# Block-sparse attention followed by a GELU layer pair: the second layer of batch 0 by seven products, casts moved between engines, and a new order of all instructions

## The chip, the cores and the metric

The kernel runs on one core of a Trainium2 chip. The core has five engines that each work through their own instructions in order: TensorE (PE in the profile) multiplies matrices into PSUM, VectorE (DVE) and ScalarE (ACT) do elementwise work, GpSimd (POOL) does elementwise work and issues some transfers, and SyncE (SP) issues most transfers. Sixteen DMA engines move data between the chip's memory and the on-chip buffers. Engines wait for each other by semaphores. The metric is the device time of one execution in microseconds; lower is better.

## The reference

The inputs are q, k and v with 4 batches, 8 heads, 768 positions and 64 dimensions, and two weight matrices, w_in (512 x 2048) and w_out (2048 x 512), all in float32.

First comes attention in which each position sees only some blocks of 64 keys. For every query the mean key of each of the 12 blocks gives a score; the three best blocks that are not in the future, and the query's own block, are kept. Inside them the mask is causal, and a softmax over the kept scores weighs the values:

```
k_rep = k.reshape(B, H, n_blocks, block, D).mean(axis=3)
gate_scores = np.einsum('bhsd,bhnd->bhsn', q, k_rep)
top_idx = np.argsort(gate_scores, axis=-1)[..., -top_k:]
scores = scale * np.matmul(q, k.transpose(0, 1, 3, 2))
```

The heads of a position are put side by side (512 numbers), which gives x with 3072 rows. Two layers follow: h = x @ w_in, g = the tanh form of GELU of h, and out = g @ w_out.

## The kernel before

The work goes batch by batch; one batch is 768 positions. Within a batch the heads are taken in pairs, p = 0 to 3 for batch 0 and 4 to 15 for batches 1 to 3.

**Preparing a pair** (`pre`, called by `prepare`). For batches 1 to 3 a pair's keys and queries are loaded by four transfers each (`load`, L427), in a layout that VectorE's 32 x 32 block transpose (L585) turns into dimension by position. For the keys VectorE then sums each block (L628) and makes ksb from the sums (L645). Keys and queries are cast to 16 bits per head by `copy`, whose lines are L391 on ScalarE, L393 on GpSimd and L395 on VectorE. TensorE multiplies queries by ksb (the gate, L693); VectorE transposes the result (L709) and selects the three best blocks (L716, L725, L726, L730). The resulting mask is transposed, by TensorE (L762) for batches 0 and 1 and by a transfer (L769) after that, and copied into extra rows of the queries, so that a score product adds the mask by itself.

**Attention of a pair** (`heads2` for batch 0, `heads` for the others). Per head and pair of key blocks, TensorE computes scores (L866 for batch 0, L1049 later), ScalarE takes the exponential (L885, L1062), GpSimd clears what lies in the future on the diagonal (L911, L1076), and TensorE multiplies by the values (L934, L1088). VectorE divides by the sums, and the result is turned into xT, by TensorE (L991) or a transfer (L996).

**First layer** (`s1`). For each of 16 groups (j, h), eight matmuls of 384 columns (L1124) give a tile of h, and ScalarE writes its GELU into G (L1136). G is stored as four quarters A11, A12, A21, A22: by halves of the hidden dimension and of the positions.

**Second layer.** For batches 1 to 3, `s2` computes G times w_out as a 2 x 2 block product with seven products of blocks in place of eight. VectorE makes sums of the quarters of G (`sums`, L1194, four for each of four slices c, into XS and, in place, A21) and of the quarters of w_out (`w_sums`, L1176, into TS and, in place, B12). For each of three token tiles TensorE runs seven products of eight matmuls with 256 columns (L1254), and VectorE combines them with five copies and additions (L1298). For batch 0, `s2_plain` computes the product directly: six token tiles of 16 matmuls with 512 columns (L1206), each copied out once by VectorE or ScalarE. Since `w_sums` changes w_out in place, its sums wait for batch 0's direct products.

**Buffers that share memory.** The first loads of batch 0 land in memory that G and TS use later, and 16-bit keys, queries and masks of batch 0 lie in XS. `early` lists what must be done before G and TS are written.

**What sets the order.** The kernel does not emit its work as written. Each piece is an `Op` with the engines that it may use and an estimated duration on each, its dependencies, the buffers that it takes and gives, and a priority. `Plan.solve` walks through time with these estimates, picks among the pieces that can start soonest the one of best priority, and chooses the engine that would end it first. The list `RANK` replaces all priorities by position. The planner's estimates decide the order only; on the chip every engine runs its own order and waits where a result is not there yet.

**Warming matmuls** (`warm`, L1401). 72 matmuls on the identity matrix, whose results nobody uses, take the lowest priority. The planner puts them where, by its estimates, TensorE would have nothing else to do.

**Weights and queues.** GpSimd issues w_in and w_out in two halves each (`load_w`, L485), each first half behind a tiny copy (L482) that waits for a certain load. SyncE has tiny loads (`hold`, L493) that wait until the first half of w_in, and later of w_out, has landed; the loads of pair 4's queries and keys stand behind the first, the other loads of batch 1 behind the second. The last operation in the kernel's own text that bears on the change is this:

```
s1(0)
s2_plain(0)
w_sums()
```

Of the kernel before, what the change touches and what calls it, by code (L numbers as in the profile page):

```python
# [21 lines left out]
    143, 420, 146, 147, 145, 418, 121, 260, 475, 56, 260, 228, 112, 261,  # L22
    587, 70, 261, 497, 19, 324, 5, 4, 324, 6, 2, 323, 8, 631, 1, 326, 32,
    54, 326, 31, 24, 324, 16, 758, 3, 329, 20, 42, 329, 13, 337, 326, 40,
    367, 372, 329, 30, 355, 38, 955, 1277, 846, 49, 934, 948, 573, 141, 248,
    583, 1191, 645, 590, 118, 241, 117, 242, 240, 198, 61, 119, 83, 613,
    108, 900, 357, 89, 751, 650, 150, 88, 253, 252, 148, 388, 1017, 1315,
    1018, 986, 109, 50, 36, 362, 473, 27, 204, 130, 22, 28, 712, 129, 23,
    21, 832, 236, 135, 265, 286, 124, 209, 428, 151, 520, 230, 325, 351,
    954, 235, 327, 350, 901, 624, 328, 433, 1099, 552, 310, 939, 305, 97,  # L30
    375, 529, 318, 882, 317, 417, 374, 889, 330, 285, 363, 287, 69, 233,
    595, 174, 137, 595, 90, 176, 339, 384, 339, 95, 111, 256, 898, 581, 441,
    280, 110, 897, 629, 923, 227, 474, 352, 298, 258, 543, 921, 62, 259,
    660, 142, 626, 829, 316, 510, 131, 216, 710, 276, 160, 26, 187, 282,
    321, 366, 189, 526, 208, 277, 533, 257, 185, 949, 431, 429, 494, 430,
    577, 331, 268, 641, 278, 838, 381, 625, 273, 289, 320, 462, 237, 465,
    369, 461, 730, 171, 464, 359, 341, 436, 458, 264, 358, 348, 1512, 269,
    456, 364, 398, 937, 213, 432, 361, 365, 360, 864, 460, 251, 219, 639,
    281, 354, 272, 347, 909, 234, 535, 344, 899, 340, 338, 370, 307, 127,
    218, 760, 387, 373, 243, 217, 791, 98, 379, 378, 945, 353, 186, 839,  # L40
    416, 478, 371, 776, 523, 956, 380, 138, 591, 524, 175, 343, 229, 488,
    170, 349, 801, 445, 840, 482, 12, 199, 65, 491, 595, 309, 564, 37, 79,
    85, 80, 84, 713, 17, 1128, 1069, 1232, 283, 284, 1228, 43, 41, 134, 313,
    1093, 1138, 1143, 1171, 755, 9, 559, 314, 400, 579, 288, 477, 466, 476,
    522, 15, 415, 444, 446, 521, 11, 1071, 504, 413, 1094, 25, 585, 512,
    602, 592, 94, 1070, 621, 841, 1072, 7, 593, 530, 528, 642, 14, 489,
    1114, 1319, 484, 10, 578, 414, 409, 485, 39, 493, 471, 454, 499, 18,
    549, 859, 861, 560, 34, 684, 734, 952, 1073, 35, 636, 596, 1102, 677,
    48, 496, 857, 447, 486, 29, 1235, 1257, 1269, 1286, 165, 1248, 778, 990,
    1198, 1220, 1217, 1218, 1223, 308, 203, 291, 211, 190, 715, 721, 1230,  # L50
    51, 172, 1226, 1266, 503, 565, 534, 681, 767, 676, 576, 822, 678, 652,
    653, 759, 770, 786, 612, 536, 911, 787, 792, 793, 800, 916, 917, 1043,
    1249, 126, 125, 222, 293, 295, 303, 292, 300, 226, 158, 689, 690, 736,
    743, 817, 836, 965, 404, 195, 192, 391, 395, 545, 546, 702, 423, 201,
    757, 421, 424, 425, 377, 691, 693, 718, 762, 735, 563, 495, 479, 505,
    541, 519, 619, 1124, 487, 194, 1237, 729, 246, 247, 245, 244, 249, 498,
    584, 427, 383, 604, 795, 794, 1061, 1213, 412, 746, 630, 932, 1321, 440,
    434, 270, 91, 907, 401, 768, 123, 634, 63, 796, 720, 104, 212, 798, 802,
    651, 675, 1040, 72, 724, 896, 46, 1044, 919, 254, 605, 223, 1039, 106,
    615, 294, 667, 744, 178, 668, 774, 924, 597, 68, 1329, 597, 87, 662,  # L60
    597, 173, 205, 52, 53, 81, 82, 77, 396, 76, 773, 989, 531, 86, 78, 918,
    74, 107, 385, 144, 221, 386, 159, 816, 664, 225, 356, 844, 833, 177,
    977, 392, 163, 692, 183, 782, 834, 301, 181, 154, 940, 835, 179, 740,
    393, 164, 705, 402, 538, 890, 335, 599, 103, 156, 599, 115, 169, 599,
    132, 162, 33, 73, 601, 616, 666, 459, 71, 688, 513, 483, 665, 719, 845,
    149, 255, 197, 188, 399, 502, 196, 714, 302, 567, 166, 726, 722, 304,
    206, 622, 75, 394, 506, 128, 717, 716, 306, 224, 765, 723, 290, 220,
    707, 403, 514, 673, 764, 537, 698, 262, 600, 96, 550, 600, 140, 334,
    600, 116, 167, 64, 555, 994, 974, 161, 263, 553, 544, 202, 184, 500,
    501, 728, 297, 59, 210, 279, 518, 152, 312, 1127, 618, 122, 1274, 1216,  # L70
    623, 136, 319, 1214, 406, 1126, 480, 368, 322, 733, 139, 1260, 457,
    1215, 938, 271, 470, 114, 661, 410, 1019, 155, 935, 481, 953, 927, 933,
    1264, 603, 790, 812, 903, 566, 250, 930, 902, 654, 426, 606, 725, 761,
    699, 1666, 872, 1341, 883, 1541, 1060, 1023, 992, 1062, 1645, 928, 904,
    922, 942, 1373, 950, 1063, 1088, 1007, 1178, 711, 685, 814, 819, 1663,
    1542, 92, 448, 905, 1067, 655, 1090, 1101, 1547, 818, 913, 910, 929,
    1394, 1064, 1032, 1029, 1068, 1139, 1056, 1053, 975, 1097, 1182, 468,
    451, 453, 925, 1049, 1013, 1059, 1066, 885, 1006, 1001, 875, 876, 101,
    1225, 914, 1356, 1425, 1275, 1100, 1112, 1255, 1227, 1137, 467, 442,
    881, 912, 1098, 1492, 1494, 1491, 1469, 1579, 1649, 804, 450, 463, 1144,  # L80
    1675, 1766, 1751, 1459, 1605, 1609, 1607, 920, 1689, 1688, 1278, 1389,
    1452, 1468, 1641, 1710, 961, 1680, 1660, 1683, 1697, 967, 737, 749, 100,
    1696, 1754, 1009, 1011, 784, 1031, 1033, 1016, 1025, 1024, 1020, 1132,
    1095, 1045, 1131, 1140, 1146, 1147, 1046, 1221, 1262, 1276, 1263, 777,
    750, 1239, 1241, 1080, 659, 656, 772, 1243, 1083, 695, 979, 57, 779,
    783, 1118, 1160, 754, 1158, 1219, 1298, 1324, 886, 1014, 1440, 1516,
    669, 511, 382, 469, 443, 1209, 570, 753, 868, 1152, 1245, 1314, 703,
    1409, 1538, 1424, 1421, 1461, 1458, 1672, 113, 267, 105, 180, 982, 1771,
    200, 982, 1772, 232, 982, 1775, 342, 299, 58, 60, 207, 67, 539, 93, 828,
    452, 397, 66, 969, 527, 848, 1351, 870, 133, 588, 1642, 1156, 988, 1212,  # L90
    1700, 1606, 991, 1429, 1699, 1698, 1092, 1057, 1010, 1048, 1608, 727,
    1581, 1455, 1578, 1177, 1244, 1532, 1496, 1175, 960, 1602, 936, 617,
    968, 1183, 1366, 1047, 157, 983, 1769, 231, 983, 1768, 756, 983, 1770,
    311, 405, 120, 274, 275, 438, 532, 408, 657, 1234, 492, 906, 435, 542,
    849, 866, 865, 644, 878, 1580, 1206, 1258, 1681, 1390, 1065, 1291, 1701,
    1682, 1194, 1159, 1740, 1026, 1717, 1190, 1419, 1021, 1661, 908, 803,
    1117, 1456, 1106, 1236, 1121, 999, 620, 998, 1089, 996, 1406, 830, 984,
    1773, 558, 984, 1774, 594, 984, 1776, 1489, 411, 437, 1724, 1723, 449,
    407, 873, 877, 884, 1332, 1204, 871, 389, 850, 966, 1005, 419, 895,
    1008, 1353, 1304, 1261, 1224, 1290, 915, 658, 1012, 1203, 1355, 780,  # L100
    1085, 1129, 855, 888, 1240, 1022, 1229, 1523, 1242, 1145, 856, 887, 788,
    1084, 825, 1030, 1289, 860, 1113, 747, 985, 1778, 556, 985, 1777, 540,
    985, 1767, 748, 1331, 1323, 1515, 1514, 1345, 820, 1346, 1526, 957, 962,
    1352, 1326, 731, 853, 1081, 1082, 672, 1252, 607, 1551, 1335, 1015,
    1201, 1561, 507, 1438, 1120, 1256, 1313, 1483, 1125, 1310, 1322, 1312,
    571, 1296, 1325, 1433, 785, 1437, 1119, 1420, 752, 1055, 1155, 1671,
    1259, 1493, 568, 569, 1270, 1272, 1422, 1684, 697, 831, 808, 869, 1611,
    943, 947, 1037, 1036, 1079, 813, 811, 810, 944, 1728, 1674, 1704, 1695,
    1714, 1104, 993, 1096, 1179, 1736, 1115, 1189, 1135, 1136, 1726, 1300,
    1308, 1306, 1318, 1676, 1170, 1168, 1165, 1172, 1721, 1207, 1635, 980,  # L110
    976, 1038, 1111, 1105, 1103, 562, 1233, 1148, 1163, 1281, 1544, 1134,
    1133, 1161, 1166, 1722, 1173, 1002, 1091, 1162, 1693, 1707, 963, 964,
# [167 lines left out]
def kernel(  # L280
# [9 lines left out]
    nc = tc.nc  # L290
    B, H, S, D = q.shape
    NBLK = S // 64
    NC = S // 128
# [8 lines left out]
    NG = 2 * (NC - 1)  # L302
    HALF = S // 2
    HD = DM // 2
    FAST = range(1, B)
    NCOLD = 18
    LAND = 3.0
    TURN = {"k": (), "q": (2, 3), "v": ()}
# [1187 lines left out]
```

## Time and profile before

| what | value |
|---|---|
| median of 3 runs | 259.65 us (258.12 to 259.68) |
| the profiled execution's own time | 259.51 us |
| its span | 257.8 us |
| TensorE busy | 250.8 us, 97%, 2530 matmuls |
| VectorE busy | 179.6 us, 70% |
| ScalarE busy | 165.2 us, 64% |
| GpSimd busy | 86.3 us, 33% |
| direct products of batch 0 (L1206) | 96 matmuls, 25.8 us busy |
| key and query casts on GpSimd (L393) | 21, of 0.862 us |
| query casts on VectorE (L395) | 15, of 0.590 us |
| query casts on ScalarE (L391) | 9, of 0.829 us |
| sums of G's quarters (L1194) | 48, of 0.55 to 0.57 us |

The span is the time from the first to the last instruction of the profiled execution; some 1.7 us lie around it. Busy time of TensorE counts overlapping matmuls once, so the mean duration of one matmul (0.379 us for 512 columns) is longer than the distance between two of them; what a stretch of matmuls costs is read from stretches in the timeline or in the chain of waits. In the stages of the run, batch 0's heads take until about 39 us, its first layer until 63 us, the heads of batch 1 with batch 0's second layer until about 99 us, batch 1's first layer until 124 us, and so on by batch; batch 3's second layer ends the run.

### The profile page before, as it was taken

How to read it: one execution, taken by the hardware profiler on the slowest of the kernel's cores; microseconds unless marked ns; L12 is line 12 of the kernel's file. 1: busy time of each engine (PE TensorE's matmuls, PEld its weight loads, DVE VectorE, ACT ScalarE, POOL GpSimd, SP SyncE). 2: the span in 40 equal slices, each digit the busy share in tenths (PEclk: the TensorE clock that was granted, in tenths of full speed). 3: DMA queues.
4: the chain of work that ended last, by engine and by line, in shares of the span. 5: the costliest groups of instructions: out<-in, count | busy, mean ns of one | idle time of the engine just before them, and what ended most of it. 6: DMA issues, size and time to landing. Idle time of an engine off the chain costs nothing.

```text
span 257.8 us, 6491 instructions
## 1 busy us (share of the span) xinstructions
PE 250.8 (97%) x2530; PEld 174.8 (68%) x2530; DVE 179.6 (70%) x523; ACT 165.2 (64%) x207; POOL 86.3 (33%) x169
## 2 busy tenths in 40 slices
PE   6799999998999999999999999999999999999997
PEld 5676776564556556556678876556778796667886
DVE  2887863318478999999999999997844462227552
ACT  2359688564789996565989587565898953664000
POOL 8754834003355676223043835100143310000000
DMA  8997898999969997899599694222011152000222
GB/s 159 218 152 161 152 215 132 186 225 185 206 132 212 161 196 159 154 188 174 86 206 194 113 215 99 66 69 51 1 75 42 41 104 83 3 0 0 84 81 84
DMA packets 134095, 32.63 MB, mean 127 GB/s; under 512 B 127696, under 2 KB 130096, under 8 KB 134064
## 3 DMA queue, kind: packets, MB, share of 16 engines
q1 hardware_dynamic: 129328, 27.62, 54.5%
q0 software_dynamic: 3136, 4.19, 10.0%
q10 hardware_dynamic: 1600, 0.39, 0.8%
q8 instruction: 20, 0.33, 0.5%
q14 instruction: 11, 0.09, 0.1%
HBM read 27.26 MB, written 6.29 MB: 130 GB/s over the span
## 4 chain that ended last, share of the span: by engine, by line
PE 71%; DMA 11%; DVE 7%; SPq 7%; ACT 2%; issue 2%; POOL 0%; DVEq 0%; ACTq 0%
PE bank L1254 21%; PE wide L1124 18%; PE wide L1049 10%; PE bank L1206 7%; SPq L427 6%; PE bank L1088 6%; DMA ksd<-in_k_dram 5%; DMA w_in<-in_moe_w_in_dram 4%; PE bank L1401 3%; PE bank L693 2%; DMA qsd<-in_q_dram 2%; PE wide L866 1%; ACT at L885 1%; PE bank L566 1%; DVE sel L725 1%
## 5 line engine op out<-in xcount | busy, mean ns | idle before, releaser
L1124 PE MATMUL wide<-xT,w_in 128*128 128x384 f16 x512 | 87.2, 326 | 0.1
L1136 ACT ACTIVATE G<-wide 128x768 f16<-128x768 f32 x64 | 51.8, 810 | 41.7 <-PE wide L1124 41.7
L1124 PEld LDWEIGHTS <-w_in 128*128 128x128 f16 x512 | 49.3, 98 | 33.2 <-issue 1.9
L1062 ACT ACTIVATE at<-wide 128x896 f16<-128x896 f32 x72 | 63.3, 917 | 10.5 <-PE wide L1049 8.1
L1076 POOL TENSOR_SCALAR_AFFINE_SELECT at<-at 128x256 f16<-128x256 f16 x72 | 31.1, 433 | 66.4 <-ACT at L1062 65.9
L1049 PE MATMUL wide<-qT,kT 76*128 76x512 f16 (+3 forms) x192 | 38.7, 305 | 0.0
L393 POOL CAST kT<-k 64x768 f16<-64x768 f32 x21 | 18.1, 862 | 37.4 <-DVE k L585 30.4
L1254 PE MATMUL bank<-w_out,G 128*128 128x256 f16 x216 | 30.0, 272 | 0.0
L1254 PEld LDWEIGHTS <-G 128*128 128x128 f16 x288 | 26.9, 98 | 4.1
L1298 DVE TENSOR_TENSOR osb<-bank,osb 128x512 f32<-128x512 f32 (+1 forms) x38 | 22.5, 596 | 8.8 <-PE bank L1254 8.2
L1206 PE MATMUL bank<-w_out,G 128*128 128x512 f16 x96 | 25.8, 379 | 0.0
L1088 PEld LDWEIGHTS <-at 128*128 128x128 f16 x504 | 21.6, 98 | 4.3 <-POOL at L1076 0.4
L885 ACT ACTIVATE at<-wide 128x1024 f16<-128x1024 f32 (+3 forms) x24 | 20.8, 917 | 5.5 <-PE wide L866 5.4
L1049 PEld LDWEIGHTS <-kT 76*128 76x128 f16 x192 | 17.5, 98 | 9.7
L1088 PE MATMUL bank<-v,at 128*128 128x65 f16 x504 | 23.8, 194 | 0.0
L1254 PEld LDWEIGHTS <-XS 128*128 128x128 f16 x216 | 20.3, 98 | 3.1 <-issue 0.3
L1254 PE MATMUL bank<-TS,XS 128*128 128x256 f16 x144 | 20.6, 272 | 0.0
L585 DVE STREAM_TRANSPOSE k<-ksd 128x768 f32<-128x768 f32 x12 | 11.6, 969 | 10.2 <-DMA ksd<-in_k_dram 10.2
L1194 DVE TENSOR_TENSOR XS<-G 128x768 f16<-128x768 f16 x12 | 6.5, 550 | 15.2 <-ACT G L1136 15.0
L1401 PE MATMUL bank<-ident 128*128 128x256 f16 x72 | 12.8, 302 | 2.1 <-DVE ident L323 2.1
L972 DVE TENSOR_TENSOR xn<-bank,zr 128x384 f16<-128x384 f32 x24 | 13.4, 558 | 0.8
L1206 PEld LDWEIGHTS <-G 128*128 128x128 f16 x96 | 8.7, 98 | 7.6 <-issue 1.0
(97 smaller groups left out, 322.8 us busy)
## 6 DMA issues: line engine op xcount, KB each, us to landing
out_dram<-osb SPq DMA_DIRECT2D x23, 256.0 KB, 2.0
vsd<-in_v_dram SPq DMA_DIRECT2D x26, 192.0 KB, 3.2
qsd<-in_q_dram SPq DMA_DIRECT2D x48, 96.0 KB, 2.5
ksd<-in_k_dram SPq DMA_DIRECT2D x48, 96.0 KB, 2.5
w_in<-in_moe_w_in_dram POOLq DMA_DIRECT2D x2, 1024.0 KB, 10.7
w_out<-in_moe_w_out_dram POOLq DMA_DIRECT2D x2, 1024.0 KB, 12.5
G<-in_k_dram SPq DMA_DIRECT2D x4, 192.0 KB, 4.6
G<-in_v_dram SPq DMA_DIRECT2D x4, 192.0 KB
```

The costliest lines, as they stand in the source:

```text
L393: nc.gpsimd.tensor_copy(out=out, in_=in_)
L885: nc.scalar.activation(out=T["at", u][:, :, 0:n], in_=plan.buf[("st",) + u].rearrange("p (h w) -> p h w", h=2)[:, :, 0:n], func=AF.Exp, bi ...
L1049: nc.tensor.matmul(st[:, x:e], kT16[i][h][0:76, s0:s0 + 128], qT16[i][h][0:76, s0 + (x - cb):s0 + (e - cb)], start=True, stop=True)
L1062: nc.scalar.activation(out=T["at", u][:, 0:n], in_=plan.buf[("st",) + u][:, 0:n], func=AF.Exp, bias=0.0, scale=SCALE)
L1076: nc.gpsimd.affine_select(out=dg, in_=dg, compare_op=ALU.is_ge, fill=0.0, base=0, pattern=[[0, 2], [1, 128]], channel_multiplier=-1)
L1088: nc.tensor.matmul(pvv[:, qc, 0:65], at[:, cb + (qc - jc) * 128: cb + (qc - jc + 1) * 128], v16[i][:, jc, h, :], start=(gi == 0 and jc == ...
L1124: nc.tensor.matmul(hps[:, 512 * e:512 * e + HALF], w_in16[:, ci, (2 * j + e) * 128: (2 * j + e + 1) * 128], T["xT", b][:, ci, HALF * h:HAL ...
L1136: nc.scalar.activation(out=G[:, :, h, j, :], in_=plan.buf["hps", b, j, h].rearrange("p (e w) -> p e w", e=2)[:, :, 0:HALF], func=AF.Gelu_a ...
L1206: nc.tensor.matmul(plan.buf["ops", b, ti], G[:, f % 2, 2 * ti // NC, f // 2, ti % (NC // 2) * 128:ti % (NC // 2) * 128 + 128], w_out16[:, ...
L1254: nc.tensor.matmul(dst[:, HD * h:HD * h + HD], FACT[m][0][:, j, t * 128:(t + 1) * 128], FACT[m][1][:, j, :], start=(clear and j == 0), sto ...
L1298: nc.vector.tensor_tensor(out=dst(), in0=src(), in1=other(), op=ALU.add)
L1401: nc.tensor.matmul(plan.buf["warm", n][:, 0:256], ident16, z, start=True, stop=True)
```

## The change

The second layer of batch 0 is computed by `s2`, as for the other batches. `s2_plain` goes, with the set `FAST` that kept the sums of G's quarters to batches 1 to 3, and the list `plain` that made the sums of w_out's quarters wait. These sums and batch 0's sums get priorities near the end of batch 0's first layer. In batches 1 to 3 key casts may run on GpSimd alone (before: VectorE or GpSimd), query casts on ScalarE or GpSimd (before: VectorE or ScalarE). `RANK` is another list, longer by 13, so all engines get a new order.

```diff
-    FAST = range(1, B)
...
-            kcs = [add({DVE: 0.56, POOL: 0.85}, kc_all(h),
+            kcs = [add({POOL: 0.85}, kc_all(h),
                        [t, old.get("k", None)], pr + 0.1) for h in range(2)]
...
-            q16s = [add({DVE: 0.56, ACT: 0.84}, q16(h), qcs + [old.get("s")],
+            q16s = [add({ACT: 0.84, POOL: 0.85}, q16(h), qcs + [old.get("s")],
                         pr + 0.1) for h in range(2)]
...
-            if j % 2 and h and b in FAST:
-                sums(b, j // 2)
+
+        for c in range(NJ // 2):
+            sums(b, c)
...
                 prev = w_sum[m, x] = add(
-                    {DVE: 0.66}, emit, [w_ready["out", x], prev] + early + plain.get(x, [])[-1:],
-                    1600 + x)
+                    {DVE: 0.66}, emit, [w_ready["out", x], prev] + early, 590.5 + 0.1 * x)
...
             prev = a_sum[b, m, c] = add(
                 {DVE: 0.55}, emit, g + [prev, x_free.get((b - 1, m, c))],
-                1000 * b + 600 + 4 * c)
-
-    def s2_plain(b):
...
+                1000 * b + 600 + 4 * c if b else 594 + 0.1 * c)
...
     s1(0)
-    s2_plain(0)
     w_sums()
+    s2(0)
```

In the new order the engines hold these instructions more or fewer than before: TensorE 168 products of 256 columns in place of 96 of 512; VectorE 16 sums of G's quarters and 12 additions of outputs more, 15 query casts, 3 key casts and 2 output copies fewer; GpSimd 13 query casts and 3 key casts more; ScalarE 2 query casts more. Lines below L305 have moved: in the changed file the sums of G's quarters are L1193, the products L1212, the additions of outputs L1256 and the warming matmuls L1359.

## The prediction

> **What bounds the kernel now.** I read the page's busy times first, then a table of busy time by stage, then the chain of waits, then TensorE's timeline around the change.
>
> In the table by stage the columns are: from and to, length, then busy time (and instructions) of PE, weight loads, DVE, ACT and POOL, then granted clock, DMA share, GB/s.
>
> ```profile
> PE 250.8 (97%) x2530; PEld 174.8 (68%) x2530; DVE 179.6 (70%) x523; ACT 165.2 (64%) x207; POOL 86.3 (33%) x169
> ...
> 39.00:63.00 24.00, 22.82 (x176) 13.88 (x173) 9.04 (x27) 14.99 (x19) 4.28 (x7) 1.00 1.16 178
> ...
> 68.00:97.00 29.00, 29.00 (x308) 16.94 (x307) 25.06 (x79) 26.02 (x34) 17.05 (x31) 1.00 0.90 180
> 97.00:124.00 27.00, 26.86 (x210) 15.76 (x209) 26.34 (x75) 16.98 (x24) 9.78 (x12) 1.00 0.87 161
> ```
>
> From 63 us on TensorE has practically no idle time; that is where the changed products lie. So work taken from TensorE there shortens the run, and a wait put there lengthens it one for one. VectorE is nearly as full from 97 us. Before 63 us there is one wait that counts:
>
> ```profile
> 43.30 13.99 DMA ksd<-in_k_dram
> 57.28 0.02 issue
> 57.31 0.99 DVE k L585
> 58.30 0.02 issue
> 58.32 0.95 DVE ks L628
> 59.28 0.46 DVE kT L395
> 59.74 0.73 DVE ksb L645
> 60.47 0.04 issue
> 60.51 0.48 PE bank L693 x8
> ...
> 63.38 3.24 PE bank L1206 x15
> ...
> 214.41 20.80 PE wide L1124 x128
> ...
> 237.18 13.32 PE bank L1254 x122
> ...
> 254.32 2.18 PE bank L1401 x20
> ```
>
> This is the chain of waits (start, length, what). The first keys of batch 1 land only at 57.3 us, 14 us after their last transfer is issued, because both halves of w_out (issued at 42.3 and 43.2 us, landed 10.5 and 14.5 us later) share the DMA engines. VectorE then needs 3.2 us until ksb, and only then can the gate product of pair 4 (L693) run. In TensorE's timeline that gate shows its wait:
>
> ```profile
> 60.51 0.48 PE L693 MATMUL bank<-q,ksb 128*32 128x160 f32 x8 [1.18 <-DVE ksb L645]
> ```
>
> TensorE works in order, so everything behind the gate waits too. Here 114 of the 128 matmuls of batch 0's first layer stand ahead of it; they hide all but 1.18 us.
>
> **The change, part by part.** The base is the profiled execution itself, 259.51 us (span 257.8); the median of the runs shown is 259.65, so I add to 259.5 and read the sum as the median. Positions come from the order of instructions on each engine in the two kernels.
>
> *Products.* Removed: 96 matmuls of 512 columns at 3.24/15 = 0.216 us, 20.74 us. Added: 168 of 256 columns at 13.32/122 = 0.1092 us, 18.34 us. Effect **-2.4 us**, on the path.
>
> *Warming matmuls* (L1401, 2.18/20 = 0.109 us each). 72 in both, but they move. Before, 20 stand behind the last real matmul, where they cost nothing. After, none does. Behind the gate of pair 4 and ahead of the last product stand 8 before and 26 after: 18 x 0.109 = **+2.0 us**. Three more stand in the first layer ahead of the gate; they lie in its wait and cost nothing.
>
> *Place of the gate.* In the new order 92 first-layer matmuls stand ahead of pair 4's gate, not 114. The 22 that moved behind it take 22 x 20.80/128 = 3.58 us. The gate's wait hid them; now TensorE reaches the gate at about 60.51 - 1.18 - 3.58 + 0.33 = 56.1 us and stands until ksb. Since the time of the gate is set by the keys, **+3.6 us** of work now lies behind it.
>
> *From keys to ksb.* Two of batch 0's factor sums (L1193 in the new file, 0.55 us) now stand between the transpose and ksb, a key cast (0.46) leaves, and ksb itself took 0.73 here, 0.15 elsewhere. Between -0.5 and +1; I take **+0.2**.
>
> *When the keys land.* The chain goes back to w_in's first half: issued by GpSimd at 27.06, landed at 36.3, then the small load that holds the queue, then queries, then keys. In the new order GpSimd reaches that issue one affine select, the cast of pair 3's queries and pair 2's value cast later. That query transpose ended at 28.7 here, so at this trace's times the issue would be 3.3 us late (28.7 + 2 casts of 0.82 = 30.4); VectorE's earlier part is somewhat shorter (two 0.48 us mask copies go to ScalarE). A better order of loads could also gain, by no more than the hole of some 1.5 us that the DMA engines have before 27 us. Ends -1.5 and +3.3; I take **+1.0**.
>
> *Clock after the wait.* TensorE would stand some 5 us. The row nearest to that is the start: after 2.07 us idle the first 14 warming matmuls took 3.17 us, 0.226 each, not 0.109. Against it, an idle time of 1.46 us at 10.3 us left the next warming matmuls at full speed. Ends 0 and 14 x 0.117 = 1.6; I take **+0.8**, the middle, as neither row is near 5 us. The Trainium skill ("TensorE: Matmul & The Clock Gate", Part 1) says the clock halves after an idle window of about 3.4 us and returns after as long a busy one, which would make it the full 1.6 or a little more. No row here shows a wait of that length.
>
> *Start of the seven products.* While VectorE waits for the keys, 14 of the 16 factor sums and all 8 weight sums (0.64 to 0.69) are queued behind that transpose. After ksb at 60.7 VectorE owes 4 sums (2.2), the selection of pair 4 (L709 to L730, 2.0), 8 weight sums (5.3) and 7 sums (3.8): 74.0 us. TensorE meanwhile has 36 first-layer matmuls (5.9), 38 products (4.2), 5 score groups (1.9), 21 value matmuls (0.6), masks, gate and 13 warming ones (2.1) until it needs the last of these, 75.2 us. In total enough, but product 5's third and fourth quarters and product 6's last come due just before their sums: waits of 0.4, 0.6 and 0.3 by adding up the rows. Ends 0 and 3; I take **+1.0**.
>
> *Later pairs.* From pair 5's gate to pair 6's VectorE has norms and joins 2.0, selection 2.0, transposes, sum, mask copy and ksb 3.4: 7.4 us. TensorE has 34 products (3.7), value and score matmuls 1.7, masks 0.3, warming 0.3 and the gate 0.4: 6.5. So 0.9 us idle; from pair 6 to 7 it is even. **+0.9**, ends 0 and 3. The casts taken from VectorE are already out of these numbers.
>
> *What costs nothing.* 18 casts (15 query, 3 key) leave VectorE, about 11 us, 16 sums and the joins of three tokens come, about 16 us less 1.4 for two output copies. TensorE has no idle time after 63 us that a faster VectorE could remove, so the relief gains nothing. GpSimd has 33% busy and takes 16 casts of 0.86, 14 us, beside them; that cover is questioned below.
>
> Sum: -2.4 + 2.0 + 3.6 + 0.2 + 1.0 + 0.8 + 1.0 + 0.9 = +7.1; 259.5 + 7.1 = **266.6 us**.
>
> **Rivals.**
>
> *The keys come early (no change, 259.8).* If SP issues the first queries and keys without the 2.88 us stall that its row shows at 38.67, the keys' packets are through before w_out's begin; a key load's median landing is 2.5 us. If they land by 52.5 us (56.1 less 3.2 of VectorE, with slack), the gate waits for nothing: -2.4 products, 21 x 0.109 = +2.3 warming, -1.2 for the old wait, +1.0 and +0.9 as above, less 0.3 for sums begun earlier, +0.3. Against it: the order queries, keys, w_out is the same as now, where they did not slip ahead. 15%.
>
> *GpSimd blocks VectorE (269.5).* Small VectorE operations stretch beside GpSimd's casts:
>
> ```profile
> 112.11 0.28 DVE L726 TENSOR_TENSOR sel<-sel,sel 128x120 f32<-128x120 f32 x1
> ...
> 118.33 0.98 DVE L726 TENSOR_TENSOR sel<-sel,sel 128x120 f32<-128x120 f32 x1
> ```
>
> The second ran beside key and value casts on GpSimd (117.44 to 120.0). Four query casts and a key cast more fall between 60 and 97 us, each able to hold up VectorE by about 0.7: up to 3 us more, where TensorE waits for VectorE: 266.6 + 2.9. For the milder case: VectorE's own casts go. The Trainium skill ("SBUF — State Buffer", Who interferes with whom) states an exclusive lock: a VectorE operation with two inputs in SBUF waits for the whole of a GpSimd instruction that reads SBUF. By it the factor sums and selections would each wait up to 0.8 us. 18%.
>
> *Faster (256).* The first: keys early, and the heads of batch 0 also end 2 us sooner, so that the first layer starts at 37.5 instead of 39.6, and the sums find VectorE idle (it has 9.0 of 24 us busy before 63 us): 259.8 - 2.1 - 1.9 = 255.8. 5%. That the change does not remove what it says is out: the orders show it.
>
> **How the numbers follow.** Forecast 62%, its own range 262.5 to 268.5 (clock, landing and start at their low or high ends together). With the early keys (258.5 to 261.5) cut at 260 and the blocked VectorE to 270, the range is 260 to 270; about 2 in 10 is left out. Bounds of 1%, about what a measurement of this kernel can tell, are 257.1 and 262.2: faster 5%; same 15% from early keys and 3% from the forecast's edge; slower the rest, 77%.
>
> **What would show it.** Right: TensorE's timeline has a wait of 4 to 6 us before pair 4's gate with 36 first-layer matmuls behind it; 168 products at 0.109 us; warming matmuls among batch 0's products; none after the last. The keys land near 58 us. Wrong: the keys landing before 53 us, which takes away 5 us of the sum at once; or an order of the first 39 us that brings w_in several microseconds sooner.

## The result and the profile after

The changed kernel takes 270.47 us (median of 4 runs, 270.09 to 271.74) against 259.44 for the kernel before (4 runs), a ratio of 1.0445 with a 95% interval of 1.0393 to 1.0496: slower, and 3.9 us above the 266.6 us that were predicted. Some executions of a kernel are slower at a lower granted clock; the ratios here leave them out, the medians do not. The profiled execution took 270.09 us (span 268.4), 10.58 more than the one before; the prediction's sum was 7.1.

The page of the changed kernel, its busy times and the granted clock in 40 slices of 6.7 us:

```profile
PE 251.5 (94%) x2602; PEld 182.2 (68%) x2602; DVE 184.1 (69%) x532; ACT 165.4 (62%) x207; POOL 97.6 (36%) x185
...
PEclk9999999995999999999999999999999999999999
```

TensorE is busy for the same time as before (251.5 and 250.8 us) in a span that is 10.6 us longer, and one slice, at about 63 us, ran at half the clock. What ends and follows the wait, in TensorE's timeline (start, length, instruction, in brackets the wait):

```profile
62.35 0.76 PE L693 MATMUL bank<-q,ksb 128*32 128x160 f32 x8 [7.69 <-DVE ksb L645]
63.05 3.74 PE L1124 MATMUL wide<-xT,w_in 128*128 128x384 f16 x12
66.62 0.60 PE L1212 MATMUL bank<-w_out,G 128*128 128x256 f16 x4
```

Pair 4's gate (0.48 us before) waits 7.69 us in place of 1.18, and the 12 first-layer matmuls behind it take 3.7 us where 12 x 0.1625 = 1.95 is their usual time. The chain of waits says what was late (start, length, what), and VectorE's timeline shows the last stretch of it:

```profile
28.80 8.21 DMA w_in<-in_moe_w_in_dram
...
44.59 13.55 DMA ksd<-in_k_dram
```

```profile
58.17 0.98 DVE L585 STREAM_TRANSPOSE k<-ksd 128x768 f32<-128x768 f32 x1 [8.95 <-DMA ksd<-in_k_dram]
59.07 0.52 DVE L1193 TENSOR_TENSOR XS<-G,XS 128x768 f16<-128x768 f16 x1
59.51 0.94 DVE L628 TENSOR_REDUCE ks<-k 128x12 f32<-128x768 f32 x1
60.36 1.20 DVE L1193 TENSOR_TENSOR G<-G 128x768 f16<-128x768 f16 x1
61.49 0.80 DVE L645 TENSOR_TENSOR ksb<-bmask,ks 128x32 f32<-128x32 f32 x1
```

The keys land 0.86 us later than before, and from there to ksb VectorE needs 4.15 us in place of 3.2: two factor sums stand between, and the second, 0.55 us elsewhere, takes 1.20 while GpSimd casts keys (59.21 to 61.16). So the gate is 1.84 us later than before, and the other 8.7 us arise behind it. Of those, 1.44 us are waits between 63 and 97 us (all from 86.4 us on, ahead of score matmuls), and 1.63 us are waits that lie much later, in batch 2's heads. There the table by stage reads, before and then after (from and to, length, busy time and instructions of PE, weight loads, DVE, ACT and POOL, clock, DMA share, GB/s):

```profile
135.00:168.00 33.00, 33.00 (x385) 24.79 (x384) 31.84 (x90) 23.82 (x31) 15.21 (x27) 1.00 0.71 135
```

```profile
135.00:168.00 33.00, 31.37 (x391) 24.61 (x389) 31.55 (x79) 25.43 (x32) 22.32 (x40) 1.00 0.83 157
```

### The profile page after: what moved, and what is told of

Read it like the earlier page. It is cut to its first block, busy times and chain, and to the rows that moved or that the text cites. A ratio compares the mean times of both kernels' runs of the same rounds, so it can differ in the third digit from the quotient of the medians.

```text
span 268.4 us, 6671 instructions
## 1 busy us (share of the span) xinstructions
PE 251.5 (94%) x2602; PEld 182.2 (68%) x2602; DVE 184.1 (69%) x532; ACT 165.4 (62%) x207; POOL 97.6 (36%) x185
## 4 chain that ended last, share of the span: by engine, by line
PE 69%; DMA 8%; DVE 7%; POOL 6%; ACT 3%; SPq 3%; issue 3%; POOLq 0%; DVEq 0%; ACTq 0%
PE wide L1124 26%; PE bank L1212 24%; PE wide L1049 7%; DMA ksd<-in_k_dram 5%; PE bank L1088 4%; DMA w_in<-in_moe_w_in_dram 3%; SPq L427 2%; PE bank L693 2%; ACT at L1062 2%; PE bank L1359 1%; PE wide L866 1%; DVE ks L628 1%; POOL at L1076 1%; DVE ksb L645 1%; POOL kT L393 1%
## 5 line engine op out<-in xcount | busy, mean ns | idle before, releaser
L1124 PE MATMUL wide<-xT,w_in 128*128 128x384 f16 x512 | 89.0, 330 | 0.0
L1212 PE MATMUL bank<-w_out,G 128*128 128x256 f16 x288 | 40.6, 272 | 0.0
L1212 PEld LDWEIGHTS <-G 128*128 128x128 f16 x384 | 36.1, 98 | 6.3 <-issue 0.3
L1256 DVE TENSOR_TENSOR osb<-bank,osb 128x512 f32<-128x512 f32 (+1 forms) x50 | 29.7, 599 | 13.4 <-PE bank L1212 12.7
L393 POOL CAST kT<-k 64x768 f16<-64x768 f32 x24 | 20.4, 850 | 26.0 <-DVE k L585 20.3
L1212 PEld LDWEIGHTS <-XS 128*128 128x128 f16 x288 | 26.6, 97 | 4.1 <-issue 0.5
L1212 PE MATMUL bank<-TS,XS 128*128 128x256 f16 x192 | 27.5, 272 | 0.0
L1193 DVE TENSOR_TENSOR XS<-G 128x768 f16<-128x768 f16 x16 | 9.5, 592 | 22.6 <-ACT G L1136 22.3
L585 DVE STREAM_TRANSPOSE k<-ksd 128x768 f32<-128x768 f32 x12 | 11.6, 969 | 9.0 <-DMA ksd<-in_k_dram 9.0
L1359 PE MATMUL bank<-ident 128*128 128x256 f16 x72 | 14.4, 299 | 2.3 <-DVE ident L323 2.3
L693 PE MATMUL bank<-q,ksb 128*32 128x160 f32 (+1 forms) x128 | 7.8, 316 | 8.8 <-DVE ksb L645 8.7
L393 POOL CAST qT<-q 64x768 f16<-64x768 f32 x13 | 10.9, 840 | 10.3 <-DVE q L585 8.2
L1212 PE MATMUL bank<-w_out,XS 128*128 128x256 f16 x96 | 14.2, 272 | 0.0
```

Source lines behind the costliest of these rows:

```text
L393: nc.gpsimd.tensor_copy(out=out, in_=in_)
L693: nc.tensor.matmul(g[32 * j:32 * j + 32, 0:32 * n].rearrange("g (c t) -> g c t", t=32), (T["ksb", p] if a == 0 else ksbx).rearrange("p h n ...
L1124: nc.tensor.matmul(hps[:, 512 * e:512 * e + HALF], w_in16[:, ci, (2 * j + e) * 128: (2 * j + e + 1) * 128], T["xT", b][:, ci, HALF * h:HAL ...
L1212: nc.tensor.matmul(dst[:, HD * h:HD * h + HD], FACT[m][0][:, j, t * 128:(t + 1) * 128], FACT[m][1][:, j, :], start=(clear and j == 0), sto ...
L1256: nc.vector.tensor_tensor(out=dst(), in0=src(), in1=other(), op=ALU.add)
L1359: nc.tensor.matmul(plan.buf["warm", n][:, 0:256], ident16, z, start=True, stop=True)
```

## The experiments

The expectations call the warming matmuls "products of zeros" (they multiply the identity). Two readings were on trial. **A:** behind the gate only TensorE counts, as the prediction's sum has it; what is taken out of TensorE's work there is won in full. **B:** VectorE, which after the keys owes 14 factor sums, 8 weight sums and a selection, has as much to do there as TensorE. Except where it is said otherwise, an edit is made in the changed kernel, mostly on the finished order (`order = plan.solve()`), which leaves all else in place. In files with added lines the line numbers are two or three higher.

The keys did not land at the same time in all profiles, although nothing touched their transfers in most of these runs. So the table has the start of the keys' transposition (L585) as well, and the time from there to the end of the span. The last column is the granted clock from 63 to 97 us; 0.05 less than 1.00 there is at most 34 x 0.05 = 1.7 us of TensorE's work. The last three columns come from one profiled execution each. e16 and e17 compute only a part of what the changed kernel computes.

| run | edit | median us | ratio to before, 95% | keys' transposition | from there to the end | clock, 63 to 97 us |
|---|---|---|---|---|---|---|
| before | | 259.44 | | 57.31 | 200.5 | 1.00 |
| after | | 270.47 | 1.0393 to 1.0496 | 58.17 | 210.2 | 0.95 |
| e1 | 36 first-layer matmuls ahead of the gate | 271.53 | 1.0405 to 1.0492 | 58.98 | 210.8 | 0.85 |
| e2 | TensorE kept busy in the wait | 269.84 | 1.0380 to 1.0412 | 59.62 | 208.6 | 1.00 |
| e3 | no warming matmuls behind the gate | 270.72 | 1.0415 to 1.0458 | 60.28 | 208.5 | 0.94 |
| e4 | query casts on VectorE again | 275.93 | 1.0607 to 1.0657 | 59.40 | 214.6 | 0.91 |
| e5 | 6 factor sums ahead of the keys | 269.83 | 1.0362 to 1.0488 | 59.86 | 208.3 | 0.96 |
| e8 | e1 and e5 | 269.34 | 1.0345 to 1.0421 | 60.11 | 207.8 | 0.90 |
| e11 | e1, e3, e5, and 4 weight sums ahead | 264.77 | 1.0179 to 1.0242 | 59.45 | 203.5 | 0.95 |
| e16 | no factor sums in batch 0 | 270.60 | 1.0384 to 1.0499 | 58.77 | 209.6 | 0.95 |
| e17 | e1, e3, e16 | 266.41 | 1.0103 to 1.0340 | 59.54 | 205.2 | 0.90 |
| e6 | keys ahead of w_out | 261.77 | 1.0062 to 1.0134 | 49.98 | 210.1 | 1.00 |
| e12 | e6 and e3 | 262.57 | 1.0106 to 1.0169 | 49.45 | 211.2 | 0.95 |
| e18 | e12, 4 weight sums on GpSimd | 268.39 | 1.0297 to 1.0415 | 50.23 | 216.7 | 0.90 |

### TensorE relieved alone: e1, e2, e3

e1, with `layer0` picking the first layer's matmuls and GELUs of batch 0:

```
gate4 = order.index(last[HP]["gate"][0])
late = [op for op in order[gate4:] if layer0(op)]
order = order[:gate4] + late + [op for op in order[gate4:] if not layer0(op)]
```

> All 36 first-layer products of batch 0 that stand behind pair 4's gate on TensorE (and the one GELU that goes with the last of them) stand ahead of it. They are 36 x 0.1625 = 5.85 us of work, and the wait at the gate was 7.69 us. Theory A (behind the keys TensorE alone sets the end, so what moves into the wait is won in full, and with a wait of some 1.8 us the clock stays up): 5.85 less, and most of the 2.07 us of the slow clock less, so 262 to 264 us against 270. Theory B (behind the keys VectorE's queue, with 10 factor sums and 8 weight sums still to come, is the next bound, and the moved products only covered it): 266 to 269 us, with new waits of TensorE for sums between 65 and 80 us.

e2, emitted directly ahead of the gate, into the gate's bank:

```
for n in range(60):
    nc.tensor.matmul(g[:, 0:256], ident16, ident16.unsqueeze(1)
                     .to_broadcast([128, 2, 128]), start=True, stop=True)
```

> 60 products of zeros without a use stand directly ahead of pair 4's gate on TensorE, 60 x 0.109 = 6.5 us, inside the wait of 7.69 us; nothing else moves. If the 2.07 us that the gate and the 12 products after it lost come from the granted clock alone: 268.0 to 268.8 us, with the gate at 0.41 and the 12 at about 1.95 us. If they were late for their data, or if VectorE's queue would hold what follows anyway: 269.8 to 270.6 us.

e3:

```
for op in order[gate4:]:
    if any(k[0] == "warm" for _, k in op.takes):
        op.emit = lambda _: None
```

> The 26 products of zeros that stand behind pair 4's gate are left out; no result uses them. Theory A (TensorE sets the end there): 26 x 0.109 = 2.8 us less, 267.2 to 268.2 us. Theory B (TensorE would wait for VectorE in their place): 269.5 to 270.6 us, with waits of TensorE for factor sums or weight sums in place of the products.

e1 took 5.85 us of work out of TensorE's path and gained nothing, so it missed both readings' numbers. TensorE's timeline of e1 shows where it went: the wait at the gate has shrunk to 1.15 us, and a new one for VectorE's selection stands behind it.

```profile
63.16 0.48 PE L693 MATMUL bank<-q,ksb 128*32 128x160 f32 x8 [1.15 <-DVE ksb L645]
...
67.80 0.71 PE L762 MATMUL bank<-ident,madd 128*128 128x128 f16 x5 [3.40 <-DVE madd L730]
68.30 1.06 PE L1212 MATMUL bank<-w_out,G 128*128 128x256 f16 x4
```

A third wait, 0.57 us for a sum of w_out's quarters, follows at 71 us; the two new ones make 3.97 us. The wait also brought the slow clock back (4 products in 1.06 us, 0.60 at full speed), as the table by stage shows:

```profile
68.00:80.00 12.00, 11.43 (x87) 8.07 (x86) 10.24 (x19) 7.22 (x10) 2.24 (x4) 0.69 0.46 83
```

At 0.69 instead of 1.00 these 12 us hold an estimated 3.7 us less work; in the changed kernel the slow clock cost 1.9 us. So, by this estimate, about two thirds of what e1 moved came back as waits for VectorE and the rest through the clock; what e1 would gain at full clock no run shows.

e3's median is no better than the changed kernel's either. But its keys came 2.1 us later, and from the keys on it is 1.7 us shorter: between A's 2.8 us and B's next to nothing. e2 shows the clock by itself:

```profile
55.49 6.71 PE L1427 MATMUL bank<-ident 128*128 128x256 f16 x60
63.80 0.48 PE L693 MATMUL bank<-q,ksb 128*32 128x160 f32 x8 [1.60 <-DVE ksb L645]
64.22 2.12 PE L1124 MATMUL wide<-xT,w_in 128*128 128x384 f16 x12
66.18 0.60 PE L1212 MATMUL bank<-w_out,G 128*128 128x256 f16 x4
```

From the gate's start to the first product 2.38 us (63.80 to 66.18), in the changed kernel 4.27 (62.35 to 66.62): the slow clock costs 1.9 us there. From the keys on e2 is 1.6 us shorter, but in its profile the keys came 1.45 us later, and the median gained only 0.6. Reading A is out for e1; of e3's 2.8 us at most 1.7 were won.

### VectorE relieved alone: e5, e16

e5 puts the last two of the first four factor sums and the second four ahead of the keys' transposition:

```
first = set(a_sum[0, m, c] for c in range(2) for m in (5, 6, 3, 7))
# and those of their inputs that stand later
order = order[:key4] + [op for op in order[key4:] if op in first] + [
    op for op in order[key4:] if op not in first]
```

> On VectorE the 6 factor sums of batch 0 that stand behind pair 4's key transposition (the last two of the first four and the second four) stand ahead of it, in the 9 us in which VectorE waits for the keys. No other engine's order changes but for three products of zeros. The three runs before this one that relieved TensorE alone gained 0 to 0.6 us; the reading tested here is that VectorE's queue from the keys to pair 5's key transposition (17.3 us of work) and TensorE's work of the same stretch both set the end, nearly level. By it: two sums and the contention between the keys and the gate go (4.15 us becomes 2.2 to 2.6), the gate comes 1.5 to 1.9 us earlier, and TensorE, full from there, lets nothing more through: 267.5 to 269 us. If TensorE alone were the bound: the same 1.5 to 1.9. If VectorE alone were: all of 6 x 0.55 + 0.65 = 4.0 us, 265.5 to 266.8 us.

e16 leaves out all 16, and lets the products read G's parts:

```
+RAW = {1: (A11,), 2: (A12,), 3: (A12,), 4: (A22,), 5: (A22,), 6: (A11,), 7: (A21,)}
-FACT[m][0][:, j, t * 128:(t + 1) * 128],
+(RAW if b == 0 else FACT)[m][0][:, j, t * 128:(t + 1) * 128],
```

> The changed kernel without the 16 factor sums of batch 0 on VectorE; products 3, 5 and 6 of that batch read parts of G directly, so its output is not the reference's. The number and place of all products stay. VectorE's queue from the keys to pair 5's key transposition is 16 - 2 sums and the stretched pieces shorter: of 17.4 to 19 us some 8 to 9 go. Reading 1 (two level queues, TensorE's not shortened): only the stretch from the keys to the gate gets shorter (4.15 to about 2.4), 267.5 to 269 us, TensorE without a wait from the gate to 85 us. Reading 2 (VectorE's queue alone sets the end; in all runs so far but one the span was 190.8 to 192.7 us after the start of pair 5's key transposition): that start at 67.5 to 69.5 us, 260.5 to 263 us.

e5's median, 269.83 us, missed the 267.5 to 269 expected from two level queues; its keys came 1.7 us later than the changed kernel's, and from the keys on it is 1.9 us shorter, as such queues should make it, and no more. e16 is the clearer one. VectorE then has 6.59 us to spare ahead of the first output sum, and the time is that of the changed kernel, 270.6 us:

```profile
68.71 0.68 DVE L1178 TENSOR_TENSOR TS<-w_out,TS 128x1024 f16<-128x1024 f16 x1
75.98 1.02 DVE L1259 TENSOR_TENSOR osb<-bank,osb 128x512 f32<-128x512 f32 x2 [6.59 <-PE bank L1214]
76.92 0.97 DVE L585 STREAM_TRANSPOSE k<-ksd 128x768 f32<-128x768 f32 x1
```

So VectorE alone does not set the end either. (That pair 5's keys' transposition, the last line, starts some 191 us ahead of the end in nearly all runs is a common mark of both queues, not a cause.) The gate came 2.85 us after the keys' transposition began (4.18 in the changed kernel), not some 2.4 as expected; the slow clock stayed and cost 0.5 us more (0.24 up to the first product, 0.27 in the first four), and the keys came 0.6 us later: so even the 1.5 us that two level queues would leave did not show in the time. From the gate to 97 us TensorE has the same three short waits as in the changed kernel: there its own work sets the pace.

### Both relieved: e8, e11, e17

> Both at once: the 6 factor sums ahead of pair 4's key transposition on VectorE, and the 36 first-layer products ahead of pair 4's gate on TensorE. If the two queues set the end together, the sum is more than the parts (0 and about 1.7): VectorE's 4.0 us, 265.5 to 267 us. If something else sets it (the landing of pair 5's tiles, ScalarE's GELUs): 268 to 270 us.

e11 adds to e8's edits e3's and this line:

```
first |= set(w_sum[m, 0] for m in (5, 6, 7, 4))
```

> As the one before it, and the four weight sums of the first half of w_out also stand ahead of pair 4's key transposition, and the products of zeros behind the gate are left out (no result uses them). VectorE's queue behind the keys is then 6 x 0.55 + 4 x 0.66 + 0.65 = 6.6 us shorter than in the changed kernel, TensorE's 36 x 0.1625 + 26 x 0.109 = 8.7 us. If the two queues set the end together: 263 to 264.5 us. If something else does from 4 us on: 265.5 to 267 us.

> As the one before it (batch 0's factor sums left out), with the 36 first-layer products ahead of pair 4's gate and without the 26 products of zeros behind it (these no result uses): both queues are shorter by 8 to 9 us. Reading 1: now all of it is won, 261 to 263 us. Reading 2: the same as the run before it, 260.5 to 263 us. If a third thing stands at 3 to 5 us (pair 5's tiles, ScalarE's exponentials): 265 to 267 us.

e8 gained 1.1 us where 3.5 to 5 were expected, a miss: its profile is 2.4 us shorter from the keys on, but the keys came 1.9 us later in it. With e11 the relief is large on both queues and the gain, 5.7 us, is nearly what was expected and more than any edit of one queue gave; from the keys on it is 6.7 us.

e17 is e1, e3 and e16 at once, and so the fairest test. Alone, these three changed the median by +1.1, +0.3 and +0.1 us, together by -4.1; from the keys on by +0.6, -1.7 and -0.6, together by -5. A sum that is so much more than its parts is the mark of two queues that set the end together. No run has e1 and e3 together without relief of VectorE, so how much of it those two alone would bring is open.

e17 takes still more work from VectorE than e11, yet was not faster: ratios 1.0221 (1.0103 to 1.0340) and 1.0211 (1.0179 to 1.0242). The table by stage shows a likely reason, e11 first:

```profile
63.00:80.00 17.00, 14.96 (x135) 11.20 (x134) 16.45 (x51) 9.62 (x13) 6.06 (x11) 0.90 0.75 153
```

```profile
63.00:80.00 17.00, 14.40 (x120) 10.32 (x119) 13.57 (x39) 9.24 (x12) 5.70 (x11) 0.80 0.73 138
```

The clock was 0.80 and not 0.90 (17 us x 0.10 = 1.7; the two profiled executions differ by 1.74): TensorE, with little to do, waited 2.19 us for the mask (1.74 in e11). e17's one execution at a mean clock of 1.00 took 263.34 us, its others, at 0.987 to 0.994, 266.38 and more. So a third limit shows behind the two queues: TensorE's own clock, in the waits that the relief opens.

### The common cause: e6, and the same in the kernel before: e7

```
 w_ready["out", x] = load_w("out", w_out16, moe_w_out, ..., [ld["q", HP]], 40,
-    None if x else ("q", HP))
+    None if x else ("k", HP))
```

> The first half of w_out waits for pair 4's keys instead of pair 4's queries, so the keys' 4 transfers have the DMA engines to themselves and land some 8 to 10 us earlier (48 to 50 us instead of 58 to 60); w_out's halves start and land some 5 us later. Nothing else moves. If the end is set by VectorE's queue from the keys on together with TensorE's: VectorE starts that queue 8 to 9 us earlier, the wait at the gate goes, and the rest moves up until w_out's sums or the GELUs are late: 260 to 263 us. If w_out, now late, takes the keys' place: 266 to 270 us, with waits of TensorE or VectorE for w_out between 60 and 70 us.

> The kernel before, with the one edit that the run above made in the changed kernel: the first half of w_out waits for pair 4's keys instead of its queries, so the keys land at about 46 instead of 57 us. There the gate waited only 1.18 us, since 114 and not 92 first-layer products stood ahead of it, and no sum of the second layer of batch 0 stands on VectorE behind the keys. If the late keys cost the changed kernel much because of what stands behind them, the same edit gains little here: 258.3 to 259.0 us (the 1.18 us go, at most). If an early landing is worth something by itself: 256 to 258 us. If w_out, later by some 3 us, is now late for the plain products: 260 us and more.

e6: 261.77 us, 8.7 us less by one word. The keys' transposition starts at 49.98 (it could have started at 46.3, when the keys had landed), and TensorE's timeline has no wait at the gate:

```profile
50.70 4.71 PE L1124 MATMUL wide<-xT,w_in 128*128 128x384 f16 x28
55.34 0.48 PE L693 MATMUL bank<-q,ksb 128*32 128x160 f32 x8
55.75 2.12 PE L1124 MATMUL wide<-xT,w_in 128*128 128x384 f16 x12
```

VectorE's queue starts 8.2 us earlier and TensorE has no wait from 39 to 77 us, so it no longer matters which of the two is longer. In the kernel before, the same edit is worth nearly nothing: 258.74 us, ratio 0.9966 (0.9932 to 1.0000), so 0 to 1.8 us. The late keys were there already; the change took away what stood in front of the gate (92 for 114 matmuls) and put 22 sums, 14 of G's quarters and 8 of w_out's, behind the keys.

### What is left: e12, e18, e4, e14, e13

> The changed kernel with pair 4's keys ahead of w_out, as in the run that gave 261.77 us, and without the 26 products of zeros behind the gate (no result uses them). In that run TensorE had no wait from 39 to 78 us and 16 of the 26 stood there. If TensorE sets the end now: 26 x 0.109 = 2.8 us less, 258.8 to 259.4 us. If VectorE's queue up to pair 5's gate is level with it (that gate began at 72.28, its keys' sums ended at 71.65, 0.6 us apart): 260.5 to 261.8 us, with a new wait of TensorE for pair 5's keys' sums or for factor sums.

e18 is e12 with the second half's weight sums moved:

```
-nc.vector.tensor_tensor(out=dst[:, js], ...)
+(nc.gpsimd if js.start else nc.vector).tensor_tensor(out=dst[:, js], ...)
```

> The changed kernel with pair 4's keys ahead of w_out and without the products of zeros behind the gate (262.57 us in the run above), and with the four weight sums of w_out's second half done by GpSimd, which is nearly idle from 57 to 70 us. If VectorE's queue was what held that run: 4 x 0.66 = 2.6 us of it go, 259.5 to 261 us. If GpSimd is slower than some 2 us a sum, or holds VectorE up while it works: 262 to 265 us, with waits of TensorE for these sums.

e12 gained nothing over e6 and missed both of its expectations. In the profile, part of the 2.8 us turned into waits for a factor sum and an output sum (0.87 and 0.30 us, at 64.7 and 68.0), and the clock fell from 80 us on. But e12's three executions at a mean clock of 1.00 took 261.93 to 262.72 us too, so the clock is not the whole of the rest. e18, some 5.7 us slower than e12, came out above even the worse of its expectations: a weight sum takes GpSimd 2.1 to 2.9 us, and VectorE's factor sums stand still meanwhile (below).

e4 and e14 try the casts, by setting the engine of the finished operations: in e4 13 query casts of the changed kernel go back to VectorE, in e14 18 casts of the kernel before go to GpSimd.

> The 13 query casts that go to GpSimd go to VectorE again, at the same places of the order; the key casts stay on GpSimd. If GpSimd's queue and its overlap with VectorE make the waits of batch 2's heads (1.63 us between 135 and 168 us) and part of those of 63 to 97 us: 268.8 to 269.5 us, with GpSimd's busy time about 97.6 - 13 x 0.85 = 87 us. If VectorE, 184 us busy, is as full there as GpSimd: 269.8 to 271.5 us.

> The part of the change that moves casts, alone: the kernel before, in its own order, with the 3 key casts and the 15 query casts that VectorE did there done by GpSimd (0.85 us for 0.55). If GpSimd's queue and its overlap with VectorE cost what batch 2's heads lost after the change: 1 to 2 us more, 260.5 to 262 us, with waits of TensorE for query rows between 130 and 170 us. If relief of VectorE is worth what the opposite move cost in the changed kernel (5.5 us for 13 casts): 255 to 258 us. If both engines have room: 259.3 to 260 us.

e4 is 5.5 us slower than the changed kernel, more than either of its expectations. The changed kernel's VectorE has no room for them (10.6 of 11 us busy from 97 us on, 25.9 of 27 from 108, 31.5 of 33 from 135). In the old order the casts' move alone made 260.23 us, ratio 1.0030 (0.9993 to 1.0067): between nothing and 1.7 us. Its profile (262.98 us; the clock is below 1.00 only ahead of 80 us) has none of the forecast waits in batch 2's heads:

```profile
135.00:168.00 33.00, 32.92 (x400) 25.01 (x397) 29.92 (x80) 24.86 (x31) 19.99 (x35) 1.00 0.77 142
```

So GpSimd's casts do not make batch 2's 1.63 us by themselves; the new order is needed for it. In the changed kernel the chain of waits runs through GpSimd's casts and its clearing of the diagonal from 142.1 to 149.6 us, then through ScalarE and VectorE until 160.8, so the casts seem to have a part in it there. Whether the order alone would do it stays open.

> The kernel before with pair 4's keys ahead of w_out and without its 28 products of zeros behind pair 4's gate; 23 of them stand in the last 18 us, where TensorE waits for other engines now and then. If they cover waits: the same time as with the keys alone. If TensorE's clock falls in the waits that they filled: up to 1 us more. If the 5 others count: 0.5 us less.

e13, the kernel before with its keys ahead of w_out and without the 28 warming matmuls behind the gate, is the fastest of all: 257.69 us, ratio 0.9939 (0.9909 to 0.9969). It beats both kernels, by 1.6 us against the one before. The step from e7 to it, 0.7 us by the ratios where 0.5 was expected, is within their intervals.

## Why the prediction was right or wrong

The direction held, and so did the first half of the mechanism: the gate stands still for keys whose landing hardly changed, and the work that used to fill the wait lies behind it. Three terms of the sum failed, and they make the 3.5 us by which it was short: the clock after the wait (+0.8, measured 1.9), the stretch from the keys to ksb (+0.2, measured 1.0), and the cover of the casts and the relief of VectorE, put at nothing (measured 1.6). The sum's premise failed too, that a change of TensorE's work behind the gate counts in full: VectorE's queue stands level with it there.

| term | forecast | in the profile after |
|---|---|---|
| products | -2.4 | -2.4 |
| warming matmuls behind the gate | +2.0 | +2.0 |
| 22 first-layer matmuls behind the gate | +3.6 | +3.6 |
| keys landing later | +1.0 | +0.9 |
| keys to ksb | +0.2 | +1.0 |
| clock after the wait | +0.8 | +1.9 |
| start of the seven products and later pairs | +1.9 | +1.4 (63 to 97 us) |
| relief of VectorE, casts on GpSimd | 0 | +1.6 (135 to 168 us) |
| not assigned | | +0.6 |

The right-hand column is the account of one profile, with the rates of its rows. It does not say what each term would give back if it were undone alone.

- **The clock** was the largest wrong size among the terms that I bounded. I took the middle between "no loss" and 1.6; e2 shows 1.9, above the upper end, so the upper end was the nearer one. The middle of two ends was a poor choice: the wait was far longer than the row with no loss (1.46) and longer than the one with a loss (2.07). It was also longer than the 4 to 6 us forecast, 7.69: TensorE came to the gate at 54.66 and not 56.1 us, as its first layer began 1.0 us sooner, and the gate came later.
- **Keys to ksb:** the two sums were counted at their lone 0.55 us each, less a cast. The 1.20 us of the second stands beside GpSimd's key casts, which the change itself had put there. I had shown such a stretched row and used it only in a rival.
- **The cover of the casts and the relief of VectorE**, put at nothing, failed in batch 2, where the stage table of before had TensorE at 33.00 of 33 us and VectorE at 31.84: little room for any stretched operation on VectorE. I had read only as far as 124 us. In the old order the casts alone did not make such waits (e14); the share of the new order is open.
- **Start of the seven products, and later pairs:** the row is near by luck. The three waits forecast for the start (+1.0) did not come; TensorE has none from the gate to 86.4 us. The later pairs cost 1.4 and not 0.9, in two waits for ScalarE's exponentials and one for a copied mask, not for VectorE's way to the gates.
- **The landing** was met, but by a profile with early keys: in the nine others with these transfers the keys' transposition began at 58.77 to 60.28 us, which would make the term 1.5 to 3.0.
- **The place of the gate** was right as a term of a sum and misleading as a cause. I had worked out that VectorE's debt ended at 74.0 us and TensorE's at 75.2, and yet priced TensorE's share as if it counted alone. By the medians e1 and e3 gave nothing, e16 gave nothing, e17 gave 4.1, e11 5.7, e6 8.7.
- **The rival "keys come early"** was priced at 259.8 us; e6, which makes it true, took 261.77. The 1.6 us of batch 2 are in it still (31.39 of 33 us busy there).
- **The rival "GpSimd blocks VectorE"** named a real thing (the 1.20 us), but it cost ahead of the gate: behind it, up to 97 us, TensorE's waits were below the forecast (1.4 for 1.9).

## What to carry to other kernels

When a late transfer releases two engines at once, add up what each owes from there to their next meeting point; if the sums are level, no edit of one engine is worth its own length (the most that one gave here, from the keys on, is 1.9 of 4.0 us), and what counts is the transfer. An order that is found anew should keep the filler ahead of the late arrival: the same late keys cost 0 to 1.8 us where 114 matmuls stood in front of the gate and no such sum behind the keys on VectorE, and 8.7 us where 92 stood in front and 22 sums behind. Of two transfers that share the DMA engines, hold the big one that is needed later until the small one that is needed first has landed.

## What the runs showed of the hardware

**Clock.** After 7.69 us of waiting, the next 4 us of matmuls ran at about half speed. The Trainium skill ("TensorE: Matmul & The Clock Gate", Part 1) has the clock at half after an idle window of some 3.4 us and until a busy window of the same length has passed; 1.9 us lost at half speed is 3.8 us of time, which agrees roughly. But losses came from shorter waits too, and there the measurement decides: waits of 1.74 (e11), 1.85 (e14), 1.97 (e8) and 2.19 us (e17) were each followed by 3 us at a clock of 0.50 to 0.64, one of 2.17 us (e18) by 3 us at 0.83, while the longest single wait that left it at 1.00 was 1.60 us (e2). In e1 the clock stayed at 0.50 for 7.4 us behind a wait of 3.40 us, with one more of 0.57 us in them. Each of these is one profile. A loss also came from two short waits (0.95 and 0.30 us in e4, followed by 0.73). In e12 TensorE waited 0.65 and 0.68 us with 0.9 us of matmuls between, and then had 3 us at a clock of 0.53 (timeline, then table by stage):

```profile
79.39 0.54 PE L1049 MATMUL wide<-qT,kT 76*128 76x512 f16 x2 [0.68 <-ACT at L1062]
```

```profile
80.00:83.00 3.00, 3.00 (x20) 1.80 (x21) 2.90 (x17) 2.58 (x4) 2.30 (x5) 0.53 0.69 109
```

In e11, e17 and e18 the same two waits left the clock at 1.00; why they differ is open. In e6 three warming matmuls stand between them, the second wait is 0.35 us, and the clock stayed up.

**VectorE beside GpSimd.** e18's timelines of GpSimd and of VectorE:

```profile
65.03 2.32 POOL L1176 TENSOR_TENSOR TS<-w_out,TS 128x1024 f16<-128x1024 f16 x1
67.32 2.43 POOL L1176 TENSOR_TENSOR w_out<-w_out 128x1024 f16<-128x1024 f16 x1
...
70.81 2.12 POOL L1176 TENSOR_TENSOR TS<-w_out,TS 128x1024 f16<-128x1024 f16 x1
```

```profile
65.41 2.36 DVE L1193 TENSOR_TENSOR XS<-XS,G 128x768 f16<-128x768 f16 x1
67.80 2.36 DVE L1193 TENSOR_TENSOR XS<-G,XS 128x768 f16<-128x768 f16 x1
...
71.02 0.96 DVE L585 STREAM_TRANSPOSE k<-ksd 128x768 f32<-128x768 f32 x1
```

VectorE's sums, 0.55 us alone, take as long as GpSimd's, one for one, while the transposition, with one input, keeps its 0.96 us beside the last. The Trainium skill ("SBUF — State Buffer", Who interferes with whom) states it as an exclusive lock: a VectorE instruction with two inputs in SBUF contends with a GpSimd instruction that reads SBUF; one with a single input, outside two fast modes, does not.

**Landing.** The start of the keys' transposition ranged from 58.17 to 60.28 us over ten profiles in which the transfers, their order and their queues were those of the changed kernel. So the landing of a transfer that shares the DMA engines with 2 MB of weights is not a fixed time; 2 us of it is as much as several of the terms above.
